# Loading q, k and v for two batches at once, nine rows per partition on all 128 partitions

## Chip, cores, metric

One core of one Trainium2 chip. The metric is device time in microseconds (us), the median of several executions. The runs of the kernel before lie within 0.22% (465.1 to 466.12 us). A run over 1.5% above the fastest of its kernel counts as slow.

## The reference

Attention with a forget gate, then a spectral mix of the result:

```python
# q, k, v: (8 batches, 8 heads, 576, 64) f32;  f: (8, 8, 576)
cum = cumsum(log(clip(f, 1e-4, 1)))
scores = q @ k^T / 8 + cum[..., :, None] - cum[..., None, :]      # causal
x = softmax(scores) @ v            # -> (8, 576, 512), heads side by side
X = rfft(x, axis=1)[:, :64]        # 64 modes
Y[m] = X[m] @ (w_r[m] + 1j * w_i[m])                # 64 x 512 x 512, twice
u = x + irfft(Y, n=576)
out = u + relu(u @ w_ch)
```

The weights `w_r` and `w_i` are 134 MB in f32, q, k and v together 28.3 MB, the output 9.4 MB. Arithmetic is in bf16.

## The kernel before

One step handles one batch and two heads; there are 32 steps. Two streams of loads run side by side. The weights come through GpSimd's software queue, which casts them to bf16 on the way (a packet that reads 2 KB is recorded with 1024 B landed), into a ring of nine tiles of 2 x 4 modes (1 MB in the ring, 2.1 MB read). q, k, v come uncast through SyncE's hardware queue, three staged steps deep.

```python
def emit_w_load(n):                       # 64 tiles in all; first half shown
    wb = wpool.tile([128, 2, MG, D], BF16, tag="wb", name="wb")
    for t, src in enumerate((moe_w_r, moe_w_i)):
        nc.gpsimd.dma_start(wb[:, t, :, :],           # rows of 512 f32: 2 KB packets
            src[g*MG:(g+1)*MG, dc*128:(dc+1)*128, :].rearrange("m p e -> p m e"))
    # ... second half of the tiles: two rows at once, 4 KB packets

def emit_loads(s):                        # RP = 96 partitions, NR = 6 rows each
    dc, b = steps[s]
    for d, src in zip(QKVst[s % STG], (q, k, v)):
        nc.sync.dma_start(d[:, :, :, :].rearrange("p h r d -> p h (r d)"),
            src[b, 2*dc:2*dc+2, :, :].rearrange("h (p r) d -> p h (r d)", r=NR))

def emit_transposes(s):                   # cast, transpose on TensorE, copy out of PSUM
    # ... K: two half-height copies into tiles whose other half is zero
    for h in range(2):
        hs = slice(h*64, h*64+64)
        nc.scalar.copy(KTz[s % NK][h][hs, 0:S].rearrange("c (p r) -> c p r", r=NR),
                       tv[hs, :, :])

# the loop over steps (attention of step s, transposes of s + 1, loads of s + 2)
if s > B:                                 # from step 9 on
    while nmode < (s - B) * NTH // (NS - B):
        emit_modes(nmode)                 # needs weight tile nmode; frees a ring slot
        nmode += 1
        next_w()                          # loads tile nmode + 8
```

After the 32 steps the kernel works through the other half of the weight tiles, and then writes the output in a tail that needs the last tile.

The softmax here doesn't subtract the row's maximum and nothing guards it: scores larger than these inputs give would overflow.

## Time and profile before

| | before |
|---|---|
| time, median | 466.04 us (465.1 to 466.12, the first 3 runs) |
| span of the profiled run | 463.0 us |
| last weight tile landed | 417.4 us |
| tail after it | 45.6 us |
| busy PE / ACT / DVE | 68% / 54% / 53% |

From the page, the span in 40 slices of 11.6 us: busy tenths of ACT and of the 16 DMA engines, and what those moved:

```profile
ACT  4789999999973675469784043442000002104763
...
DMA  8999999999999999999999999999999999982667
GB/s 205 268 268 268 268 268 268 267 267 267 268 266 228 232 258 240 246 217 264 208 206 208 211 212 211 211 211 211 211 211 211 211 211 211 211 161 83 225 245 267
```

The DMA engines are busy to 90% or more in every slice from the second to 405 us, and to 80% or more in the slice in which the weights end, near 417 us. The GB/s line counts what lands; the weights land as half of what was read, so 211 GB/s of weights alone are 422 GB/s read.

The chain that ended last, its pieces around the end of the weights (start, length, what):

```profile
402.75 14.67 DMA wb<-in_moe_w_i_dram
417.46 0.55 PE A L130 x14
418.46 0.61 PE pl L674 x4
...
456.34 1.11 DVEq L784
```

The last matmuls of the modes start 40 ns after the last landing (402.75 + 14.67 = 417.42). From there PE, ACT and DVE write the output until the span ends. Before it, the chain is nearly all landings of weights and channel weights (88% of the span is DMA).

Two stretches, with busy time of each engine, granted clock of TensorE (1 is full speed), DMA share and GB/s landed. The DMA share here adds up packet durations; it goes over 1 because packets overlap in an engine:

```profile
core 0: us, PE busy (x) PEld busy (x) DVE busy (x) ACT busy (x) POOL busy (x), PEclk, DMA share, GB/s
30.00:130.00 100.00, 84.28 (x1538) 66.29 (x1539) 89.52 (x244) 95.09 (x148) 14.83 (x20) 0.97 1.16 268
230.00:250.00 20.00, 16.12 (x329) 13.76 (x326) 15.09 (x44) 14.71 (x24) 5.95 (x8) 0.91 1.24 206
```

Between 30 and 130 us ACT is busy 95% of the time, so attention is close to being bound by ACT there. But the list of waits (total, number, longest) shows who waits afterwards:

```profile
PE A L130 <- DMA wb<-in_moe_w_i_dram: 74.2, 37, 3.5
...
PE A L130 <- DMA wb<-in_moe_w_r_dram: 27.0, 21, 1.6
```

PE waits 101 us for weights. A faster attention would reach these waits earlier.

The q/k/v issues (bytes each and median time to landing), the two queues (packets, MB, share of 16 engines' time), and three groups of work that the change touches (busy us, mean ns of one):

```profile
stq<-in_q_dram SPq DMA_DIRECT2D x32, 288.0 KB, 9.2
stk<-in_k_dram SPq DMA_DIRECT2D x32, 288.0 KB, 8.8
stv<-in_v_dram SPq DMA_DIRECT2D x32, 288.0 KB, 8.7
```

```profile
q0 software_dynamic: 51760, 67.64, 82.4%
q1 hardware_dynamic: 24960, 37.77, 25.7%
```

```profile
L407 ACT COPY KTz<-tp 64x576 bf16<-64x576 bf16 x64 | 42.9, 671 | 7.5 <-PE tp L398 6.6
...
L383 ACT CAST kb<-stk 96x768 bf16<-96x768 f32 x32 | 26.3, 834 | 0.0
...
L453 PE MATMUL ps<-QTs,KTz 128*128 128x448 bf16 x64 | 21.9, 399 | 0.0
```

**What one packet costs.** The trace also records every DMA packet, with queue, size, start and duration. I cut the stretch in which both queues work into slices of 4 us and solved by least squares for the two numbers that make (weight packets x cost + q/k/v packets x cost) fill 4 us of an engine (counts are means over the 16 engines):

```
before: packet kind           packets per engine   ns of an engine   us in all
  weights, 2 KB read                 2080               80              167
  weights, 4 KB read                 1024              156              160
  q, k, v, 1536 B                    1152               73.2             84
recorded durations of a q/k/v packet: 65 ns with no weights about, 78 ns next to weights
```

Cost and duration differ because packets overlap in an engine (the DMA share above is 1.16). The three sums, 411 us, are the 417 us in which DMA is busy, less the start (the first weight packet starts at 3.8 us) and the 4-byte packets of both queues: 4016, one for each transfer in each engine, three quarters of them 22 ns long. I call these completion packets.

### The profile page before, as it was taken

Reading aid. Unit: us, or ns where it says so; the run is one execution under the profiler, and the core shown is the slowest. Engines: PE = TensorE matmul, PEld = TensorE weight load, DVE = VectorE, ACT = ScalarE, POOL = GpSimd, SP = SyncE. Lnnn points to the kernel's source line nnn. Section 1 sums busy time; section 2 is a strip of 40 time slices with the busy share of each in tenths; the row PEclk is TensorE's granted clock in tenths of the full one; section 3 lists DMA queues with packets and bytes.
Section 4 is the critical chain, followed back from the end, with each engine's and each line's share of the span. In section 5 each row is a group of like instructions: output and inputs, shape, how many; then the busy total and the mean of one; then the engine's idle time right before and its main releaser. Section 6 shows DMA issues by size and latency. Waiting matters only on the chain.

```text
span 463.0 us, 11454 instructions
## 1 busy us (share of the span) xinstructions
PE 315.8 (68%) x4845; PEld 224.3 (48%) x4845; DVE 245.0 (53%) x625; ACT 248.0 (54%) x376; POOL 120.9 (26%) x154
## 2 busy tenths in 40 slices
PE   1768778898865673677977599996222248347993
PEld 1446556777654553556766456663122125223441
DVE  7868889999954563358777313321000012105774
ACT  4789999999973675469784043442000002104763
POOL 6111101221112211121222322322322233101884
PEclk9979999999987887579899599998555558657998
DMA  8999999999999999999999999999999999982667
GB/s 205 268 268 268 268 268 268 267 267 267 268 266 228 232 258 240 246 217 264 208 206 208 211 212 211 211 211 211 211 211 211 211 211 211 211 161 83 225 245 267
DMA packets 76852, 106.28 MB, mean 230 GB/s; under 512 B 4032, under 2 KB 55744, under 8 KB 76800
## 3 DMA queue, kind: packets, MB, share of 16 engines
q0 software_dynamic: 51760, 67.64, 82.4%
q1 hardware_dynamic: 24960, 37.77, 25.7%
q8 instruction: 38, 0.62, 0.5%
q10 hardware_dynamic: 80, 0.13, 0.2%
q14 instruction: 14, 0.11, 0.1%
HBM read 163.73 MB, written 9.44 MB: 374 GB/s over the span
## 4 chain that ended last, share of the span: by engine, by line
DMA 88%; PE 6%; ACT 1%; issue 1%; DVE 1%; POOL 1%; DVEq 0%; ACTq 0%; POOLq 0%
DMA wb<-in_moe_w_i_dram 69%; DMA wb<-in_moe_w_r_dram 12%; DMA wch<-in_moe_w_ch_dram 8%; PE pz L703 2%; PE pu L715 1%; PE pz L715 1%; ACT uo L731 1%; PE pu L698 1%; PE pl L678 1%; ACT uo L728 0%; POOL wb L87 0%; DVE uo L732 0%; DVE uo L725 0%; DVEq L784 0%; PE pl L674 0%
## 5 line engine op out<-in xcount | busy, mean ns | idle before, releaser
L130 PE MATMUL A<-XT,wb 128*128 128x16 bf16 x2048 | 77.1, 172 | 101.8 <-DMA wb<-in_moe_w_i_dram 74.2
L130 PEld LDWEIGHTS <-wb 128*128 128x128 bf16 x2048 | 68.4, 100 | 115.3 <-DMA wb<-in_moe_w_i_dram 79.2
L460 ACT ACTIVATE E<-ps 128x1024 bf16<-128x1024 f32 (+1 forms) x128 | 105.6, 855 | 19.1 <-PE ps L453 17.6
L453 PE MATMUL ps<-QTs,KTz 128*128 128x64 bf16 (+4 forms) x384 | 73.1, 303 | 8.7 <-ACT E L460 7.6
L145 DVE TENSOR_TENSOR YT<-A,Yacc 128x128 bf16<-128x128 f32 x24 | 8.8, 368 | 97.1 <-PE A L130 97.1
L87 POOL DMA_DIRECT2D wb<-in_moe_w_r_dram x32 | 24.5, 766 | 113.1 <-DMA wb<-in_moe_w_r_dram 40.0
L487 PE MATMUL pav<-va,E 128*128 128x65 bf16 x960 | 48.1, 202 | 2.8 <-DVE x_all L496 2.0
L407 ACT COPY KTz<-tp 64x576 bf16<-64x576 bf16 x64 | 42.9, 671 | 7.5 <-PE tp L398 6.6
L475 DVE TENSOR_TENSOR E<-E,trimask 128x256 bf16<-128x256 bf16 (+2 forms) x128 | 38.6, 307 | 11.5 <-ACT E L460 10.6
L633 ACT CAST yy<-pyw 128x512 bf16<-128x512 f32 x8 | 4.7, 586 | 74.0 <-PE pyw L626 74.0
L487 PEld LDWEIGHTS <-E 128*128 128x128 bf16 x960 | 41.0, 104 | 5.5 <-DVE x_all L496 2.5
L453 PEld LDWEIGHTS <-KTz 128*128 128x128 bf16 x384 | 32.3, 104 | 21.3 <-issue 14.6
L87 POOL DMA_DIRECT2D wb<-in_moe_w_i_dram x32 | 23.9, 747 | 69.3 <-DMA wb<-in_moe_w_i_dram 68.1
L621 ACT CAST XW<-pxw 128x512 bf16<-128x512 f32 x40 | 22.7, 587 | 35.1 <-PE pxw L614 35.1
L99 POOL DMA_DIRECT2D wb<-in_moe_w_r_dram x33 | 22.7, 687 | 67.7 <-DMA wb<-in_moe_w_r_dram 50.0
L614 PE MATMUL pxw<-wch,yy 128*128 128x512 bf16 x160 | 38.5, 393 | 0.0
L99 POOL DMA_DIRECT2D wb<-in_moe_w_i_dram x33 | 23.0, 697 | 53.0 <-DMA wb<-in_moe_w_i_dram 50.5
L729 POOL TENSOR_TENSOR uo<-uo 64x512 f32<-64x512 f32 (+1 forms) x14 | 25.2, 1811 | 28.6 <-DVE uo L725 25.7
L389 DVE TENSOR_TENSOR vb<-stv,wdec 96x768 bf16<-96x768 f32 x32 | 30.4, 950 | 3.4 <-PE tp L398 3.4
L418 ACT COPY VT<-tp 128x576 bf16<-128x576 bf16 x32 | 20.3, 635 | 20.4 <-PE tp L398 20.3
L496 DVE TENSOR_TENSOR x_all<-pav,rcp 128x384 bf16<-128x384 f32 x64 | 31.0, 484 | 0.5
L413 DVE COPY QTs<-tp 128x576 bf16<-128x576 bf16 x32 | 24.1, 752 | 5.3 <-PE tp L398 4.1
(103 smaller groups left out, 496.4 us busy)
## 6 DMA issues: line engine op xcount, KB each, us to landing
wb<-in_moe_w_r_dram POOLq DMA_DIRECT2D x63, 512.0 KB, 20.3
wb<-in_moe_w_i_dram POOLq DMA_DIRECT2D x63, 512.0 KB, 20.6
stq<-in_q_dram SPq DMA_DIRECT2D x32, 288.0 KB, 9.2
stk<-in_k_dram SPq DMA_DIRECT2D x32, 288.0 KB, 8.8
stv<-in_v_dram SPq DMA_DIRECT2D x32, 288.0 KB, 8.7
out_dram<-uo SPq DMA_DIRECT2D x16, 512.0 KB, 3.1
out_dram<-uo SPq DMA_DIRECT2D x7, 128.0 KB, 2.4
wch<-in_moe_w_ch_dram POOLq DMA_DIRECT2D x1, 512.0 KB, 38.0
```

What stands on the lines that cost most here:

```text
L87: nc.gpsimd.dma_start(wb[:, t, :, :], src[g * MG : (g + 1) * MG, dc * 128 : (dc + 1) * 128, :].rearrange("m p e -> p m e"),)
L99: nc.gpsimd.dma_start(wb[:, t, ms, :], src[g * M2 : (g + 1) * M2, D // 2 : D, :][ms].rearrange("m (p r) e -> p m (r e)", r=2),)
L130: nc.tensor.matmul(A[:, eb, mi, :], lhsT=wb[:, t, mi, r * D + eb * 128 : r * D + (eb + 1) * 128], rhs=XT3[:, m, c0 : c0 + 2 * B], start=(i ...
L389: nc.vector.tensor_tensor(vb[:, :, :, :], stv_[:, :, :, :].rearrange("p h r d -> p r h d"), _strided(wdec6[:, 0, c0 : c0 + 1], [[BH, NR], ...
L407: nc.scalar.copy(KTz[s % NK][h][hs, 0:S].rearrange("c (p r) -> c p r", r=NR), tv[hs, :, :],)
L453: nc.tensor.matmul(ps[:, h, o : o + n], lhsT=KTz[s % NK][h][:, jb * 128 : (jb + 1) * 128], rhs=QT[s][:, jb * 128 + c0 : jb * 128 + c0 + n] ...
L460: nc.scalar.activation(E[:, :, piece * 512 : piece * 512 + w], ps[:, :, 0:w], ACT.Exp, scale=scale,)
L475: nc.vector.tensor_tensor(dg, dg, tr, ALU.mult)
L487: nc.tensor.matmul(pav[:, i, h, :], lhsT=E[:, h, c : c + 128], rhs=va[:, jb, h, :], start=(jb == 0), stop=(jb == sb),)
L496: nc.vector.tensor_tensor(x_all[:, b, sbs[0] : sbs[0] + n, dc * 128 : (dc + 1) * 128].rearrange("p c (h d) -> p c h d", h=2), pav[:, 0:n, ...
L614: nc.tensor.matmul(pxw[:, :], lhsT=xT[:, eb, sb * 128 : (sb + 1) * 128], rhs=wch[:, eb, :], start=(eb == 0), stop=(eb == NDC - 1),)
L729: nc.gpsimd.tensor_tensor(o_sb, o_sb, u_sb, ALU.add)
```

## The change

Intent: use all 128 partitions in loads, casts and transposes, fetch longer runs, and halve the number of loads. A pair of steps now shares one load per tensor: two heads (64 partitions each, nine rows a partition) of two batches. After the transposes the batches lie on the two partition halves. So K need not be padded with zeros, and scores become matmuls of 64 rows. Staging takes the same room (two pairs instead of three steps).

```diff
-    RP = 96
+    RP = 64
     NR = S // RP
+    RG = ((0, 5), (5, 4))
-    STG = 3
+    STG = 2
@@ loads
-            dc, b = steps[s]
-            for d, src in zip(QKVst[s % STG], (q, k, v)):
+            dc, bp, _ = steps[2 * pr]
+            for d, src in zip(QKVst[pr % STG], (k, q, v)):
+                one = src[2 * bp, 2 * dc, :, :]
                 nc.sync.dma_start(
-                    d[:, :, :, :].rearrange("p h r d -> p h (r d)"),
-                    src[b, 2 * dc : 2 * dc + 2, :, :].rearrange(
-                        "h (p r) d -> p h (r d)", r=NR
-                    ),
+                    d[:, :, :, :].rearrange("p b r d -> p b (r d)"),
+                    bass.AP(tensor=one.tensor, offset=one.offset,
+                        ap=[[NR * Dh, 128], [H * S * Dh, 2], [1, NR * Dh]]),
                 )
@@ scores (cut)
-                        lhsT=KTz[s % NK][h][:, jb * 128 : (jb + 1) * 128],
-                        rhs=QT[s][:, jb * 128 + c0 : jb * 128 + c0 + n],
+                        lhsT=KTs[pr % 2][bs, h, jb * 128 : (jb + 1) * 128],
+                        rhs=QT[pr][bs, h, jb * 128 + c0 : jb * 128 + c0 + n],
@@ the loop
-            if s + STG - 1 < NS:
-                emit_loads(s + STG - 1)
-            if s + 1 < NS:
-                emit_transposes(s + 1)
+            pr, h = s // 2, s % 2
+            if h == 0 and pr + STG < NPR:
+                emit_loads(pr + STG)
+            if pr + 1 < NPR:
+                emit_transposes(pr + 1, ("kq", "v")[h])
 # cut: prologue (decay factors in the new layout), casts and copies per pair,
 # attention's output and transforms for two batches
```

More of the change, by code (lines that the diff above doesn't have):

```diff
@@ L160 @@
         qtp = actx.enter_context(tc.tile_pool(name="qtp", bufs=2))
-        vap = actx.enter_context(tc.tile_pool(name="vap", bufs=3))
+        vap = actx.enter_context(tc.tile_pool(name="vap", bufs=2))
         epl = actx.enter_context(tc.tile_pool(name="epl", bufs=1))
@@ L179, with emit_loads @@
         wdec = ssb.tile([128, NSB, BH], BF16, name="wdec")
-        wdec6 = ssb.tile([RP, NR, BH], BF16, name="wdec6")
-        NK, NE = 2, 2
+        wdec9 = ssb.tile([128, NR, B, NDC], BF16, name="wdec9")
+        NE = 2
         QKVst = [
-            [stq.tile([RP, 2, NR, Dh], F32, name=f"st{nm}{i}") for nm in "qkv"]
+            [stq.tile([128, 2, NR, Dh], F32, name=f"st{nm}{i}") for nm in "qkv"]
             for i in range(STG)
         ]
-        VTs = [kt.tile([128, SP], BF16, name=f"VT{i}") for i in range(2)]
-        KTz = [
-            [kt.tile([128, SP], BF16, name=f"KTz{i}_{h}") for h in range(2)]
-            for i in range(NK)
-        ]
-        Es = [epl.tile([128, 2, EW], BF16, name=f"E{i}") for i in range(NE)]
-        steps = [(dc, b) for dc in range(NDC) for b in range(B)]
-        def emit_loads(s):
-            dc, b = steps[s]
-            for d, src in zip(QKVst[s % STG], (q, k, v)):
-                nc.sync.dma_start(
-                    d[:, :, :, :].rearrange("p h r d -> p h (r d)"),
-                    src[b, 2 * dc : 2 * dc + 2, :, :].rearrange(
-                        "h (p r) d -> p h (r d)", r=NR
+        VTs = [kt.tile([128, 2, SP], BF16, name=f"VT{i}") for i in range(2)]
+        KTs = [kt.tile([128, 2, SP], BF16, name=f"KT{i}") for i in range(2)]
+        Es = [epl.tile([128, 2, EW], BF16, name=f"E{i}") for i in range(NE)]
+        steps = [(dc, bp, h) for dc in range(NDC) for bp in range(B // 2) for h in (0, 1)]
+        NPR = len(steps) // 2
+        def emit_loads(pr):
+            dc, bp, _ = steps[2 * pr]
+            for d, src in zip(QKVst[pr % STG], (k, q, v)):
+                one = src[2 * bp, 2 * dc, :, :]
+                nc.sync.dma_start(
+                    d[:, :, :, :].rearrange("p b r d -> p b (r d)"),
+                    bass.AP(
+                        tensor=one.tensor,
+                        offset=one.offset,
+                        ap=[[NR * Dh, 128], [H * S * Dh, 2], [1, NR * Dh]],
                     ),
@@ L224 @@
         nc.sync.dma_start(ft[:], f.rearrange("b h s -> (b h) s"))
-        for s in range(STG - 1):
-            emit_loads(s)
+        for pr in range(STG):
+            emit_loads(pr)
         nc.gpsimd.memset(trimask[:, :], 1.0)
@@ L254 @@
         for t in VTs:
-            nc.vector.memset(t[:, S:SP], 0.0)
-        for pair in KTz:
-            nc.vector.memset(pair[0][64:128, :], 0.0)
-            nc.vector.memset(pair[1][0:64, :], 0.0)
-            nc.vector.memset(pair[0][0:64, S:SP], 0.0)
-            nc.vector.memset(pair[1][64:128, S:SP], 0.0)
+            nc.vector.memset(t[:, :, S:SP], 0.0)
+        for t in KTs:
+            nc.vector.memset(t[:, :, S:SP], 0.0)
         for t in Es:
@@ L266 @@
         nc.scalar.activation(lf[:], ft[:], ACT.Ln)
-        onesS = scratch(BH, S)
+        wide = scratch(128, 2 * S)
+        onesS = wide[:BH, 0:S]
         nc.vector.memset(onesS[:], 1.0)
@@ L278 @@
             )
-        cum6_ps = psT.tile([RP, NR, BH], F32, tag="tr", name="cum6_ps")
-        for r in range(NR):
-            nc.tensor.transpose(
-                cum6_ps[:, r, :],
-                _strided(cum[:, r : r + 1], [[NR, RP]]),
-                ident_f[:BH, :BH],
+        cum2 = wide[:BH, :].rearrange("c (r h p) -> c r h p", r=NR, h=2)
+        for h in range(2):
+            nc.vector.tensor_copy(
+                cum2[:, :, h, :], _strided(cum[:, 0:1], [[1, NR], [NR, RP]])
             )
@@ L313 @@
         nc.vector.memset(wdec[64:128, 4, :], 0.0)
-        bias6 = ftf[:RP, 0 : NR * BH].rearrange("p (r c) -> p r c", r=NR)
-        nc.vector.tensor_tensor(
-            bias6[:, :, :],
-            _strided(Rb[:RP, :], [[0, NR], [1, BH]]),
-            cum6_ps[:, :, :],
-            ALU.subtract,
-        )
-        nc.scalar.activation(wdec6[:, :, :], bias6[:, :, :], ACT.Exp)
+        bias9 = ftf[:, 0 : NR * B * NDC].rearrange(
+            "p (r b c) -> p r b c", r=NR, b=B
+        )
+        for r0, n in RG:
+            cum9_ps = psT.tile([128, 5, BH], F32, tag="tr", name="cum9_ps")
+            for r in range(r0, r0 + n):
+                nc.tensor.transpose(
+                    cum9_ps[:, r - r0, :],
+                    cum2[:, r, :, :].rearrange("c h p -> c (h p)"),
+                    ident_f[:BH, :BH],
+                )
+            for h in range(2):
+                hs = slice(h * 64, h * 64 + 64)
+                nc.vector.tensor_tensor(
+                    bias9[hs, r0 : r0 + n, :, :],
+                    _strided(Rb[hs, h : h + 1], [[0, n], [H, B], [2, NDC]]),
+                    _strided(
+                        cum9_ps[hs, 0, h : h + 1], [[BH, n], [H, B], [2, NDC]]
+                    ),
+                    ALU.subtract,
+                )
+        nc.scalar.activation(wdec9[:, :, :, :], bias9[:, :, :, :], ACT.Exp)
         def emit_basis():
@@ L331, in emit_basis @@
             nc.vector.tensor_copy(m_f[:], m_i[:])
-            ang = scratch(128, 2, NSB, NM)
+            ang = wide[:, 0 : 2 * NSB * NM].rearrange(
+                "p (a b c) -> p a b c", a=2, b=NSB
+            )
             rnd = scratch(128, 2, NSB, NM)
@@ L375 @@
         QT, vaugs = {}, {}
-        def emit_transposes(s):
-            stq_, stk_, stv_ = QKVst[s % STG]
-            dc, b = steps[s]
-            c0 = b * H + 2 * dc
-            kb = qkb.tile([RP, NR, 2, Dh], BF16, tag="kb", name="kb")
-            kv = kb[:, :, :, :].rearrange("p r h d -> p h r d")
-            nc.scalar.copy(kv, stk_[:, :, :, :])
-            qb = qkb.tile([RP, NR, 2, Dh], BF16, tag="qb", name="qb")
-            nc.vector.tensor_copy(
-                qb[:, :, :, :].rearrange("p r h d -> p h r d"), stq_[:, :, :, :]
-            )
-            vb = qkb.tile([RP, NR, 2, Dh], BF16, tag="vb", name="vb", bufs=1)
-            nc.vector.tensor_tensor(
-                vb[:, :, :, :],
-                stv_[:, :, :, :].rearrange("p h r d -> p r h d"),
-                _strided(wdec6[:, 0, c0 : c0 + 1], [[BH, NR], [1, 2], [0, Dh]]),
-                ALU.mult,
-            )
-            for which, src in (("k", kb), ("q", qb), ("v", vb)):
-                tp = psT.tile([128, NR, RP], BF16, tag="tr", name="tp")
-                for r in range(NR):
-                    nc.tensor.transpose(
-                        tp[:, r, :],
-                        src[:, r, :, :].rearrange("p h d -> p (h d)"),
-                        ident_bf[:RP, :RP],
-                    )
-                tv = tp[:, :, :].rearrange("c r p -> c p r")
-                if which == "k":
-                    for h in range(2):
-                        hs = slice(h * 64, h * 64 + 64)
-                        nc.scalar.copy(
-                            KTz[s % NK][h][hs, 0:S].rearrange("c (p r) -> c p r", r=NR),
-                            tv[hs, :, :],
-                        )
-                elif which == "q":
-                    QTs = qtp.tile([128, S], BF16, tag="QT", name="QTs")
-                    nc.vector.tensor_copy(
-                        QTs[:, :].rearrange("c (p r) -> c p r", r=NR), tv
-                    )
-                    QT[s] = QTs
-                else:
-                    nc.scalar.copy(
-                        VTs[s % 2][:, 0:S].rearrange("c (p r) -> c p r", r=NR), tv
-                    )
@@ new lines, in emit_transposes, with rows @@
+        def emit_transposes(pr, what):
+            dc, bp, _ = steps[2 * pr]
+            for which in what:
+                st = QKVst[pr % STG]["kqv".index(which)]
+                sb = qkb.tile([128, NR, 2, Dh], BF16, tag="cb", name=which + "b")
+                flat = sb[:, :, :, :].rearrange("p r b d -> p b r d")
+                if which == "k":
+                    nc.scalar.copy(flat, st[:, :, :, :])
+                elif which == "q":
+                    nc.vector.tensor_copy(flat, st[:, :, :, :])
+                    QT[pr] = qtp.tile([128, 2, S], BF16, tag="QT", name="QTs")
+                else:
+                    nc.vector.tensor_tensor(
+                        sb[:, :, :, :],
+                        st[:, :, :, :].rearrange("p b r d -> p r b d"),
+                        _strided(
+                            wdec9[:, 0, 2 * bp, dc : dc + 1],
+                            [[B * NDC, NR], [NDC, 2], [0, Dh]],
+                        ),
+                        ALU.mult,
+                    )
+                for r0, n in RG:
+                    tp = psT.tile([128, 5, 2, RP], BF16, tag="tr", name="tp")
+                    for r in range(r0, r0 + n):
+                        nc.tensor.transpose(
+                            tp[:, r - r0, :, :].rearrange("c h p -> c (h p)"),
+                            sb[:, r, :, :].rearrange("p b d -> p (b d)"),
+                            ident_bf[:, :],
+                        )
+                    tv = tp[:, 0:n, :, :].rearrange("c r h p -> c h p r")
+                    def rows(t):
+                        return t.rearrange("c h (p r) -> c h p r", r=NR)[
+                            :, :, :, r0 : r0 + n
+                        ]
+                    if which == "k":
+                        nc.scalar.copy(rows(KTs[pr % 2][:, :, 0:S]), tv)
+                    elif which == "q":
+                        nc.vector.tensor_copy(rows(QT[pr][:, :, :]), tv)
+                    else:
+                        nc.scalar.copy(rows(VTs[pr % 2][:, :, 0:S]), tv)
@@ L422, in emit_vback @@
         def emit_vback(s):
-            dc, b = steps[s]
-            c0 = b * H + 2 * dc
+            dc, bp, h = steps[s]
+            c0 = 2 * bp * H + 2 * dc + h
             vp = psT.tile([128, NSB, 2, Dh], BF16, tag="tr", name="vp")
@@ L427, in emit_vback @@
                 nc.tensor.transpose(
-                    vp[:, sc, :, :].rearrange("p h d -> p (h d)"),
-                    VTs[s % 2][:, sc * 128 : (sc + 1) * 128],
+                    vp[:, sc, :, :].rearrange("p b d -> p (b d)"),
+                    VTs[s // 2 % 2][:, h, sc * 128 : (sc + 1) * 128],
                     ident_bf[:, :],
@@ L435, in emit_vback @@
                 va[:, :, :, Dh : Dh + 1],
-                _strided(wdec[:, 0, c0 : c0 + 1], [[BH, NSB], [1, 2], [1, 1]]),
+                _strided(wdec[:, 0, c0 : c0 + 1], [[BH, NSB], [H, 2], [1, 1]]),
             )
@@ L450, in emit_scores @@
             ps = psS.tile([128, 2, 512], F32, tag="sc", name="ps")
-            for h in range(2):
-                for jb, c0, n, o in PIECES[piece]:
+            h, pr = s % 2, s // 2
+            for jb, c0, n, o in PIECES[piece]:
+                for b in range(2):
+                    bs = slice(b * 64, b * 64 + 64)
                     nc.tensor.matmul(
-                        ps[:, h, o : o + n],
-                        lhsT=KTz[s % NK][h][:, jb * 128 : (jb + 1) * 128],
-                        rhs=QT[s][:, jb * 128 + c0 : jb * 128 + c0 + n],
+                        ps[:, b, o : o + n],
+                        lhsT=KTs[pr % 2][bs, h, jb * 128 : (jb + 1) * 128],
+                        rhs=QT[pr][bs, h, jb * 128 + c0 : jb * 128 + c0 + n],
                         start=True,
@@ L477, in emit_av @@
         def emit_av(s, sbs):
-            dc, b = steps[s]
+            dc, bp, hd = steps[s]
             E = Es[s % NE]
@@ L496, in emit_av @@
             nc.vector.tensor_tensor(
-                x_all[:, b, sbs[0] : sbs[0] + n, dc * 128 : (dc + 1) * 128].rearrange(
-                    "p c (h d) -> p c h d", h=2
-                ),
+                x_all[
+                    :,
+                    2 * bp : 2 * bp + 2,
+                    sbs[0] : sbs[0] + n,
+                    dc * 128 + hd * Dh : dc * 128 + (hd + 1) * Dh,
+                ].rearrange("p b c d -> p c b d"),
                 pav[:, 0:n, :, 0:Dh],
@@ L503, in emit_av, with emit_dft @@
             )
-        def emit_dft(s):
-            dc, b = steps[s]
+        def emit_dft(pr):
+            dc, bp, _ = steps[2 * pr]
             if dc == 2:
                 return
-            for c, d0, st in [(dc, dc * 128, 1)] if dc < 2 else [(2, 256, 2), (3, 257, 2)]:
-                if b == 0:
-                    XT3s[c] = xtpool.tile(
-                        [128, NM, 3 * B], BF16, tag="XT3", name=f"XT{c}"
-                    )
-                px = psT.tile([128, NM, 2], F32, tag="tr", name="px")
-                for sb in range(NSB):
-                    nc.tensor.matmul(
-                        px[:, :, :],
-                        lhsT=_strided(x_all[:, b, sb, d0 : d0 + 1], [[st, 128]]),
-                        rhs=bas[:, sb, :, :],
-                        start=(sb == 0),
-                        stop=(sb == NSB - 1),
-                    )
-                XT3 = XT3s[c]
-                nc.vector.tensor_copy(
-                    _strided(XT3[:, 0, B + b : B + b + 1], [[3 * B, NM], [B, 2]]),
-                    px[:, :, :],
-                )
-                nc.scalar.mul(XT3[:, :, b : b + 1], px[:, :, 1:2], -1.0)
+            forms = [(dc, dc * 128, 1)] if dc < 2 else [(2, 256, 2), (3, 257, 2)]
+            for b in (2 * bp, 2 * bp + 1):
+                for c, d0, st in forms:
+                    if b == 0:
+                        XT3s[c] = xtpool.tile(
+                            [128, NM, 3 * B], BF16, tag="XT3", name=f"XT{c}"
+                        )
+                    px = psT.tile([128, NM, 2], F32, tag="tr", name="px")
+                    for sb in range(NSB):
+                        nc.tensor.matmul(
+                            px[:, :, :],
+                            lhsT=_strided(x_all[:, b, sb, d0 : d0 + 1], [[st, 128]]),
+                            rhs=bas[:, sb, :, :],
+                            start=(sb == 0),
+                            stop=(sb == NSB - 1),
+                        )
+                    XT3 = XT3s[c]
+                    nc.vector.tensor_copy(
+                        _strided(XT3[:, 0, B + b : B + b + 1], [[3 * B, NM], [B, 2]]),
+                        px[:, :, :],
+                    )
+                    nc.scalar.mul(XT3[:, :, b : b + 1], px[:, :, 1:2], -1.0)
         NS = len(steps)
@@ L541 @@
         tc.no_sync_barrier()
-        emit_transposes(0)
+        emit_transposes(0, "kqv")
         for s in range(NS + 1):
-            if s + STG - 1 < NS:
-                emit_loads(s + STG - 1)
-            if s + 1 < NS:
-                emit_transposes(s + 1)
+            pr, h = s // 2, s % 2
[3 more added lines that the diff above has]
+                emit_transposes(pr + 1, ("kq", "v")[h])
             if s < NS:
@@ L560 @@
             if s >= 1:
-                emit_dft(s - 1)
                 vaugs.pop(s - 1)
+                if h == 0:
+                    emit_dft(pr - 1)
             if s > B:
```

## The prediction

> **What bounds the kernel now.** DMA, until 417 us of a 463 us span. The chain of waits is 88% DMA, nearly all landings of the weight tiles `wb`; its last DMA piece ends at 417.4 us, then a 46 us tail of PE, ACT and DVE follows. The slices show DMA at 9 tenths throughout. The stage windows show ACT busy 14.7 of 15 us between 60 and 120 us, so attention is close to ACT-bound there; but after 135 us PE waits for weights (74 us on `moe_w_i`, list of waits), so a faster attention only waits longer.
>
> So the time is DMA work before the last weight lands, plus the tail. From the DMA packet records, by queue and size:
> - weights, 2 KB read, 2080 packets per DMA engine. Alone (230-250 us) they land 204.5 GB/s, 80 ns a packet per engine: 167 us.
> - weights, 4 KB read, 1024 per engine, 209.8 GB/s, 156 ns: 160 us.
> - q, k, v: 1536 B, 18432 packets, 1152 per engine. From 15 to 135 us the two queues alternate packet for packet (1101 against 1101 per 10 us), 150 ns a pair, so 70 ns a q/k/v packet: 81 us.
>
> Sum 408 us plus a start at 3.8 us: 412, near the 417 seen.[...]
>
> **What changes on that path.** Bytes do not change (28.3 MB of q, k, v). Packets become 2304 B, 768 per engine. Packet durations before are nearly constant: 1536 B takes 65 ns alone, 78 ns when it alternates with a weight packet; the packets of f, 2304 B too, take 93 ns alone. So 28 ns for 768 B more, and the rest is fixed per packet. Estimate: 70 + 28 = 98 ns, times 768 = 75 us instead of 81: 5 us less. Half as many loads also means 48 fewer completion packets per engine, about 20 ns each: up to 1 us.
>
> A rival: 96 partitions[...]; then the gain would be larger[...]. The constant durations speak against contention, so I give it little weight.
>
> **What changes off that path.** Per pair of steps, K's four half-height copies (671 ns each) become two full-height ones (about 1.3 us in all, estimate), the casts of K go from 2 x 834 ns to about 1.2 us: ACT saves about 0.9 us of 6 us a step, DVE about 0.5. Scores in 64-row tiles shorten PE (73 us of score matmuls), which isn't limiting. Attention will run about 5 us a step instead of 6 until weights hold it up; modes begin near 65 us instead of 78. Then PE waits more for weights. The weight ring should not run dry: before, its first nine tiles had landed only at 96 us. The prologue grows by 1-2 us, hidden by DMA. The tail is untouched.
>
> **Prediction.** 466 - 5.5 = 460.5 us, range 456 to 464.5. Faster by over 2%: 0.13; same: 0.83; slower: 0.04.
>
> **What would show it.** DMA at 9 tenths until 405-415 us; last weight landing 5-6 us earlier; tail still 45-46 us; q/k/v packets about 104 ns when they alternate; ACT busy time down by about 30 us; PE's waits on weights up by tens of us.
>
> **What would make it wrong.** [...]Cost proportional to bytes: no change. DMA gaps, where the bigger, burstier loads leave attention late and the ring full: slower. A tail that moves with the granted clock.

The sums stand as 167 + 160 + 81 = 408 us, with the start 412 us; and 466 - 5.5 = 460.5 us, the 5.5 being 5 us of q/k/v packets and part of the up to 1 us of completion packets. The rival's point is that a load costs more on 96 partitions than on 128. "The constant durations" are those of the q/k/v packets: 17623 of 18432 took 78 ns.

## The result

| | before | after |
|---|---|---|
| time, median | 465.95 us (4 runs) | 458.7 us (458.57 to 458.98, 4 runs) |
| span of the profiled run | 463.0 | 457.1 |
| last mode matmuls start | 417.46 | 411.26 |
| from there to the end | 45.6 | 45.8 |
| busy ACT / DVE / PE, us | 248.0 / 245.0 / 315.8 | 227.8 / 235.6 / 311.7 |

The ratio is 0.9855 (95% interval 0.984 to 0.9869). Ratios are the mean time of one kernel's fast runs over that of the other's of the same rounds, so not quite the ratio of the medians quoted. This is 1.45% less, within the 2% that I called "same". The result is right.

The same lines of the kernel after. (Its tiles are named by the order q, k, v but loaded in the order k, q, v, so `stq` holds k.) First the slices:

```profile
ACT  3699999898836536573872133442000012005772
...
DMA  8999999999999999999999999999999999972677
GB/s 229 275 294 294 294 294 283 275 274 274 274 252 239 276 218 273 215 223 206 207 207 208 211 211 211 211 211 211 211 211 211 211 211 212 212 143 93 219 253 264
```

DMA is still full until the slice in which the weights end. The landed rate in the slices with most q/k/v rose from 268 to 294 GB/s.

```profile
396.48 14.73 DMA wb<-in_moe_w_i_dram
411.26 0.56 PE A L131 x14
412.26 0.61 PE pl L694 x4
...
450.30 1.11 DVEq L804
```

```profile
30.00:130.00 100.00, 80.95 (x1452) 61.41 (x1450) 86.36 (x233) 89.10 (x129) 15.32 (x20) 0.98 1.14 282
230.00:250.00 20.00, 14.33 (x303) 11.40 (x299) 13.57 (x40) 9.73 (x16) 5.61 (x8) 0.89 1.23 207
```

```profile
PE A L131 <- DMA wb<-in_moe_w_i_dram: 71.8, 33, 4.8
...
PE A L131 <- DMA wb<-in_moe_w_r_dram: 26.2, 21, 3.4
```

The last landing is 6.2 us earlier and the tail is as long as before. ACT has 6 us less to do between 30 and 130 us, yet PE waits for weights as long as before, 98 us.

```profile
stq<-in_k_dram SPq DMA_DIRECT2D x16, 576.0 KB, 9.2
stk<-in_q_dram SPq DMA_DIRECT2D x16, 576.0 KB, 7.9
stv<-in_v_dram SPq DMA_DIRECT2D x16, 576.0 KB, 8.4
```

```profile
q0 software_dynamic: 51760, 67.64, 83.8%
q1 hardware_dynamic: 18048, 37.77, 24.0%
```

```profile
L397 ACT CAST kb<-stq 128x1152 bf16<-128x1152 f32 x16 | 18.8, 1177 | 8.2 <-PE tp L414 8.2
...
L466 PE MATMUL ps<-QTs,KT 64*128 64x448 bf16 x64 | 13.4, 390 | 0.0
...
L427 ACT COPY KT<-tp 128x640 bf16<-128x640 bf16 x16 | 12.3, 766 | 9.7 <-PE tp L414 9.7
L427 ACT COPY KT<-tp 128x512 bf16<-128x512 bf16 x16 | 11.9, 745 | 5.2 <-PE tp L414 5.2
```

The packets:

```
q/k/v packets          per engine   ns of an engine   us in all   duration (no weights / next to weights)
before, 1536 B            1152           73.2           84.4          65 / 78 ns
after,  2304 B             768          101.3           77.8          93 / 106 ns
```

The q/k/v packets take 6.6 us less of every DMA engine, and the last weight lands 6.2 us earlier. That is nearly all of the gain.

### The profile page after: what moved, and what is told of

Same layout as the page of the kernel before. It is cut to its first block, busy times and chain, and to the rows that moved or that the text cites. A ratio compares the mean times of both kernels' runs of the same rounds, so it can differ in the third digit from the quotient of the medians.

```text
span 457.1 us, 10986 instructions
## 1 busy us (share of the span) xinstructions
PE 311.7 (68%) x4704; PEld 213.6 (47%) x4704; DVE 235.6 (52%) x592; ACT 227.8 (50%) x329; POOL 121.1 (26%) x154
## 4 chain that ended last, share of the span: by engine, by line
DMA 88%; PE 6%; ACT 1%; issue 1%; DVE 1%; POOL 1%; DVEq 0%; ACTq 0%; POOLq 0%
DMA wb<-in_moe_w_i_dram 66%; DMA wb<-in_moe_w_r_dram 13%; DMA wch<-in_moe_w_ch_dram 8%; PE pz L723 2%; PE pu L735 2%; PE pz L735 1%; ACT uo L751 1%; PE pu L718 1%; PE pl L698 1%; ACT uo L748 0%; POOL wb L88 0%; DVE uo L752 0%; DVE uo L745 0%; DVEq L804 0%; PE pl L694 0%
## 5 line engine op out<-in xcount | busy, mean ns | idle before, releaser
L131 PE MATMUL A<-XT,wb 128*128 128x16 bf16 x2048 | 72.1, 172 | 98.4 <-DMA wb<-in_moe_w_i_dram 71.8
L473 ACT ACTIVATE E<-ps 128x1024 bf16<-128x1024 f32 (+1 forms) x128 | 104.0, 873 | 26.9 <-PE ps L466 26.0
L131 PEld LDWEIGHTS <-wb 128*128 128x128 bf16 x2048 | 63.3, 99 | 113.7 <-DMA wb<-in_moe_w_i_dram 76.3
L466 PE MATMUL ps<-QTs,KT 64*128 64x64 bf16 (+4 forms) x384 | 51.2, 304 | 7.6 <-ACT E L473 6.8
L500 PEld LDWEIGHTS <-E 128*128 128x128 bf16 x960 | 39.8, 104 | 10.8 <-issue 6.4
L88 POOL DMA_DIRECT2D wb<-in_moe_w_i_dram x32 | 24.1, 753 | 71.4 <-DMA wb<-in_moe_w_i_dram 65.0
L427 ACT COPY KT<-tp 128x640 bf16<-128x640 bf16 (+1 forms) x32 | 23.0, 755 | 14.9 <-PE tp L414 14.9
L466 PEld LDWEIGHTS <-KT 64*128 64x128 bf16 x384 | 18.0, 96 | 20.8 <-issue 10.8
L542 DVE CAST XT<-px 128x128 bf16<-128x128 f32 x32 | 20.8, 808 | 9.0 <-PE px L534 8.8
L546 ACT ACTIVATE XT<-px 128x64 bf16<-128x64 f32 x32 | 14.6, 467 | 20.1 <-DVE XT L542 17.6
L634 PEld LDWEIGHTS <-yy 128*128 128x128 bf16 x160 | 15.1, 100 | 19.5 <-DVE yy L630 5.9
```

The costliest lines, as they stand in the source:

```text
L88: nc.gpsimd.dma_start(wb[:, t, :, :], src[g * MG : (g + 1) * MG, dc * 128 : (dc + 1) * 128, :].rearrange("m p e -> p m e"),)
L131: nc.tensor.matmul(A[:, eb, mi, :], lhsT=wb[:, t, mi, r * D + eb * 128 : r * D + (eb + 1) * 128], rhs=XT3[:, m, c0 : c0 + 2 * B], start=(i ...
L427: nc.scalar.copy(rows(KTs[pr % 2][:, :, 0:S]), tv)
L466: nc.tensor.matmul(ps[:, b, o : o + n], lhsT=KTs[pr % 2][bs, h, jb * 128 : (jb + 1) * 128], rhs=QT[pr][bs, h, jb * 128 + c0 : jb * 128 + c ...
L473: nc.scalar.activation(E[:, :, piece * 512 : piece * 512 + w], ps[:, :, 0:w], ACT.Exp, scale=scale,)
L500: nc.tensor.matmul(pav[:, i, h, :], lhsT=E[:, h, c : c + 128], rhs=va[:, jb, h, :], start=(jb == 0), stop=(jb == sb),)
```

## Experiments

The theory, N: the time is the sum of DMA packets up to the last weight plus a fixed tail, and a q/k/v packet next to weights costs a fixed amount besides its bytes, so fewer packets are the gain. From the two costs above: (101.3 - 73.2) ns for 768 B is 36.6 ns per 1000 B, which leaves 17 ns fixed. Rival P: a packet costs more on 96 partitions than on 128, whatever the mechanism, and 128 partitions are the gain. Rival C: the lighter attention arithmetic is the gain.

### e1: the kernel after with packets as small as before

```diff
-                    d[:, :, :, :].rearrange("p b r d -> p b (r d)"),
+                    d[:, :, :, :].rearrange("p b r d -> p (b r d)").rearrange("p (c e) -> p c e", c=3),
-                        ap=[[NR * Dh, 128], [H * S * Dh, 2], [1, NR * Dh]],
+                        ap=[[384, 128], [128 * 384, 3], [1, 384]],
```

> The kernel after, but each load fetches its bytes as 1536 B packets (three per partition) on all 128 partitions: 1152 packets per DMA engine as before, wrong result on purpose. Theory N (number of packets: a fixed cost of some 16 ns for each q/k/v packet next to a weight packet; 73 ns for 1536 B, 101.5 ns for 2304 B): the whole gain goes, last weight landing near 417 us, 464 to 466 us. Rival P (96 partitions[...], 128 cure it): stays at 458.7 us. Rival C (the lighter attention arithmetic gives the gain): stays at 458.7 us.

Measured: 465.32 us against 465.32 for the kernel before (ratio 0.9998, interval 0.9981 to 1.0015). A packet cost 72.8 ns. The hardware queue's line and the end of the weights:

```profile
q1 hardware_dynamic: 24192, 37.77, 25.4%
```

```profile
417.75 0.56 PE A L131 x14
```

The whole gain is gone, with all of the change's arithmetic and all 128 partitions still in place. Both rivals fall for this kernel: partitions are worth 73.2 - 72.8 = 0.4 ns a packet, 0.5 us in all, and the arithmetic nothing that shows.

### e2: the kernel after with packets twice as large

```diff
-                        ap=[[NR * Dh, 128], [H * S * Dh, 2], [1, NR * Dh]],
+                        ap=[[1152, 128], [1, 1152]],       # and a flat destination
```

> The kernel after, each load as one 4608 B packet per partition: 384 packets per engine, wrong result on purpose. Theory N: 187 ns each, 72 us instead of 78, so about 6 us less than the kernel after: 452.5 us (451 to 454). Rivals P and C: 458.7 us.

Measured: 453.36 us (ratio 0.9746). A packet cost 186.9 ns, 71.8 us in all; the straight line through the other two sizes gives 101.3 + 3 x 28.1 = 185.6 ns.

```profile
q1 hardware_dynamic: 11904, 37.77, 22.6%
```

```profile
405.48 0.56 PE A L131 x14
```

The kernel obeys the packet count further than the change took it. Its output is wrong, which doesn't matter for the time. A right kernel with such loads would need another layout (18 rows per partition).

### e3: the kernel before with half its packets

```diff
-                    d[:, :, :, :].rearrange("p h r d -> p h (r d)"),
+                    d[:, :, :, :].rearrange("p h r d -> p (h r d)"),
-                        "h (p r) d -> p h (r d)", r=NR
+                        "h (p r) d -> (h p) (r d)", r=2 * NR
```

> The kernel before, all its arithmetic and 96 partitions, each load as one 3072 B packet per partition instead of two of 1536 B, wrong result on purpose. Theory N: 576 packets of 130 ns, 75 us instead of 84: about 8.7 us less than before, 457.3 us (456 to 459). Rivals P and C: 466 us as before.

Measured: 459.62 us (ratio 0.9878, interval 0.9859 to 0.9896). This misses the expected range by 0.6 us but is 5.7 us faster than before, on 96 partitions and with the old arithmetic. A packet cost 132.0 ns instead of 130 (76.0 us in all), and between 8 and 16 us the packets filled only about 87% of the DMA engines' time, some 1 us more. Why 2 ns more is not settled; 96 partitions may have a small part in it.

### e4: the kernel before with the packets of the kernel after

```diff
-            [stq.tile([RP, 2, NR, Dh], F32, name=f"st{nm}{i}") for nm in "qkv"]
+            [stq.tile([128, 768], F32, name=f"st{nm}{i}") for nm in "qkv"]
-                    d[:, :, :, :].rearrange("p h r d -> p h (r d)"),
+                    d[:, 0:576],
-                        "h (p r) d -> p h (r d)", r=NR
+                        "h (p r) d -> (h p) (r d)", r=9
 # the arithmetic reads [96, 768] of the tile; columns 576 on are set to zero once
```

> The kernel before, all its arithmetic, with the packets of the kernel after: 2304 B on 128 partitions, still one load per step and tensor, wrong result on purpose. Theory N: 78.5 us of q/k/v instead of 84: 460 us (459 to 461). Rival P: 458.7 to 460 us. Rival C: 466 us.

Measured: 458.68 us, where the kernel after has 458.7 (ratio to before 0.9863). A packet cost 101.7 ns. The time is 0.3 us below the expected range, at the lower end of what rival P would give here, so this run doesn't tell N from P; e1, e2 and e3 do. The end of the weights:

```profile
411.14 0.56 PE A L130 x14
```

The load alone, with every bit of the old arithmetic, gives the whole gain. e1 and e4 together close the question for rival C.

### e5 and e6: one queue instead of two

What is the fixed cost of 17 ns? The durations suggest a place: 65 or 93 ns alone, exactly 13 more (78, 106) next to weights. Do the two queues take turns packet by packet? The counts fit that: from 45 to 55 us of the kernel after, 923 records of the weights' queue stand against 925 of the other (891 and 866 without the 4-byte completion packets). Equal counts alone would also fit turns of several packets each; but 96% of the q/k/v packets of the kernel before (17623 of 18432) had the 78 ns of one next to weights, so I take it that nearly every one has a weight packet beside it. The order itself was not shown. Theory A: the cost is paid at that alternation. In one queue, I expected, the packets of a load come in runs.

```diff
-                nc.sync.dma_start(
+                nc.gpsimd.dma_start(
@@ weights: three tiles first, then one a step, then the channel weights
-        for n in range(NRING):
+        for n in range(NFIRST):        # NFIRST = 3
@@ loop
+            if NFIRST + s < NRING:
+                emit_w_load(NFIRST + s)
 # e6 besides: staging tiles in BF16, so that the DMA casts
```

> The kernel after, with q, k, v issued from GpSimd like the weights, so that all packets stand in one queue and come in runs instead of alternating (right result; the first weight tiles are spread over the first steps so that q, k, v do not queue behind all nine). Theory A (the fixed 16 ns of a q/k/v packet is paid where an engine changes between the queues): a 2304 B packet falls from 101.5 to about 90 ns, 69 us instead of 78, last weight landing near 402 us, 450 us (448 to 453). Rival I (the cost belongs to packets that are not cast, in whatever order): 458.7 us. Rival S ([...]a blocked load holds back weights): gaps in the DMA, slower than 458.7 us.

> As the run before, and the DMA casts q, k, v to bf16 as it does the weights (v is then rounded once more; else a right result). Theory A and rival I both give about 90 ns for a packet that reads 2304 B and 450 us; where the run before stays at 458.7 us and this one falls to 450 us, rival I is right. Rival S: gaps and slower.

Measured: e5 459.39 us, e6 457.48 to 459.7 in three fast runs; both results right. e6's profiled run was slow (533.57 us at a granted clock of 1.0); I have no explanation and draw nothing from it after 250 us. The expected 450 us were missed, but not because the packets stayed dear: 4608 B (one record holds two 2304 B pieces here) cost 177 ns, 88.5 a piece instead of 101.3, and e6's cast pieces 90.5. q/k/v took 68 us, 10 less than after. (459.39 us is also the number of rival I; the cost of an uncast packet, and e7 below, speak against it.)

Not all of these 10 us belong to the queue, for the records also became larger. e2 had records of 4608 B too, as many as e5, in their own queue, and there one cost 186.9 ns. So larger records explain 6 of the 10 us (77.8 to 71.8), and the one queue the other 4. The durations agree: before any weights came, e2's records took 178 ns as a rule, and next to weights 191 (5822 of 6144); in one queue 178 is the rule again, in two thirds of e5's records. So most of the 13 ns that a neighbour in the other queue adds are gone.

e5's window from 82 to 102 us, and GpSimd's timeline, show where the 10 us went (columns as above; in the timeline start and length in us, then the wait before it):

```profile
82.00:102.00 20.00, 16.98 (x300) 13.05 (x298) 17.43 (x49) 18.32 (x27) 6.08 (x9) 0.93 0.75 202
```

```profile
63.97 0.77 POOL L568 DMA_DIRECT2D wch<-in_moe_w_ch_dram  x1 [0.44 <-DMA stv<-in_v_dram]
66.62 0.70 POOL L198 DMA_DIRECT2D stq<-in_k_dram  x1 [1.88 <-ACT VT L431]
...
81.53 0.70 POOL L198 DMA_DIRECT2D stk<-in_q_dram  x1 [4.05 <-DVE qb L399]
...
89.02 0.70 POOL L198 DMA_DIRECT2D stq<-in_k_dram  x1 [1.62 <-ACT kb L397]
93.56 0.72 POOL L198 DMA_DIRECT2D stk<-in_q_dram  x1 [3.84 <-DVE qb L399]
94.70 0.75 POOL L88 DMA_DIRECT2D wb<-in_moe_w_r_dram  x1 [0.42 <-PE tp L414]
```

The DMA share is 0.75 there, against 1.1 to 1.2 elsewhere. All nine weight tiles and the channel weights had been issued by 64 us; until the first modes freed a slot at 94.7 us, GpSimd had only q/k/v loads to issue, which wait for attention. The ring was full too early: a gap of my own making.

### e7 and e8: one queue, weights spread out

```diff
-        NFIRST = 3
+        NFIRST = 2
@@ loop
-            if NFIRST + s < NRING:
-                emit_w_load(NFIRST + s)
+            if h == 0 and nload < NRING + nmode:
+                next_w()
 # channel weights at step 20; e8: cast in the DMA, three staged pairs
```

> The one-queue kernel (q, k, v uncast, from GpSimd), with the weight tiles spread: two at first, then one every second step until the ring is full, and the channel weights at step 20. In the first one-queue run a 4608 B pair of q/k/v packets cost 177 ns per engine (68 us in all, 10 us less than the kernel after), but the DMA stood mostly idle from 82 to 102 us, because all nine tiles had landed before the first modes freed a slot, which gave some 10 us back. Theory A: without that gap the last weight lands near 401 us and the time is 449 us (447 to 453). If the 10 us are lost elsewhere[...], 455 to 460 us with other gaps.

> The same with the cast in the DMA, and three staged pairs instead of two, since they take half the room. 90.5 ns a packet, 69.5 us: 450 us (448 to 454) if there are no gaps. It tells whether deeper staging closes what gaps the other run still has.

Measured: e7 451.07 us (450.24 to 456.63, ratio 0.9723), e8 451.31 us (450.93 to 452.32, ratio 0.971, interval 0.9692 to 0.9727); both results right. e7's window at the same place:

```profile
82.00:102.00 20.00, 18.68 (x372) 14.66 (x370) 17.75 (x52) 17.51 (x26) 8.14 (x11) 0.75 1.21 237
```

The gap is closed, the last modes start at 403.6 us in both, and both kernels beat before and after (but e2, with two queues and as few records, by only 2 us: 453.36 us, last modes at 405.48): e8 is 7.4 us below the kernel after and steadier than e7. e7's slowest run is the profiled one; its granted clock was 0.686 and its tail 51 us instead of 46.

### e9, e10, e11: does the change matter in one queue?

If theory A holds, the nine-row load has little to save in one queue. So I gave the kernel before one queue.

```diff
 # e9: the kernel before, 96 partitions, 1536 B pieces
-                nc.sync.dma_start(
+                nc.gpsimd.dma_start(
 # and weights spread as in e7
```

> The kernel before (96 partitions, six rows, all its arithmetic) with q, k, v issued from GpSimd, and the weight tiles spread as in the faster one-queue kernels; right result. If the fixed cost belongs to alternating queues (theory A), a 1536 B packet costs here about 61 ns instead of 73, some 70 to 72 us in all, nearly the same as with 2304 B, and the time is 453 us (451 to 456): most of what nine rows gain disappears, because the cost they saved is not there. If the cost belongs to each q/k/v packet whatever the order, it stays near 465 us, 7 us or more behind the one-queue kernel of nine rows at 451 us, or more with gaps.

Measured: 488.15 us, slower than before (ratio 1.05); its two fast runs 480.96 and 486.53 us (the other two, near 490, count as slow by the rule of 1.5%). A clear miss: 4608 B of q/k/v cost about 270 ns instead of 177 (254 if a weight packet is held at the 80 ns of the other runs). Their durations were spread (a quarter under 191 ns, a quarter over 295), where e7 has 178 ns in over three quarters of its records. I took spread durations for a sign of contention, and rival P came back. Two more runs separate 96 partitions from small pieces.

```diff
 # e10: e7 with 1536 B pieces on 128 partitions (the edit of e1)
 # e11: e9 with 2304 B pieces on 128 partitions (the edit of e4)
```

> The faster one-queue kernel (nine-row arithmetic), its loads fetched as 1536 B pieces on 128 partitions, wrong result on purpose. In the kernel before with one queue, 4608 B of q/k/v cost an engine 270 ns with durations spread from 178 to over 320, against a nearly constant 178 for the nine-row one. If the 96 partitions do that[...]: here 178 to 190 ns, 451 to 453 us. If the 1536 B pieces do it: about 270 ns, and 480 us or more.

> The kernel before with all its arithmetic, one queue, weights spread as in the run that was slow, but 2304 B on 128 partitions, wrong result on purpose. If the 96 partitions were the cause: constant durations, 178 ns per 4608 B, 451 to 454 us. If its arithmetic or its 96 smaller loads were the cause: slow as before, 480 us or more. If the 1536 B pieces were: 451 to 454 here, and slow in the other run.

Measured: e10 453.0 us (184.7 ns per 4608 B, so 61.6 a piece), e11 454.29 us (about 186 ns; a few stalls blur this fit). The upper end of e11's range was 454. e9 and e11 in the same stretch:

```profile
120.00:240.00 120.00, 79.19 (x1369) 65.97 (x1377) 66.03 (x175) 68.72 (x96) 47.25 (x67) 0.74 1.18 232
```

```profile
120.00:240.00 120.00, 85.34 (x1676) 70.40 (x1674) 76.13 (x206) 77.87 (x112) 52.02 (x78) 0.81 1.18 249
```

The DMA engines are equally busy, and e9 lands less. Against e7, small pieces on 128 partitions cost 2 us in one queue (e10; three of them share a record of 4608 B, so there are no more records), and the old arithmetic 3 us (e11). Neither comes near e9's 30 us, so 96 partitions are what is left to make e9 slow. No run has 96 partitions with larger pieces in one queue, so a need for both together isn't excluded. Nor does any run show by what mechanism 96 partitions would do it; measured is the cost, 270/184.7 = 1.46 times that of e10's equal pieces.

All runs (uncast pieces in the shared queue are joined in records of 4608 B; the others are records of their own):

| run | load, queue | ns per piece | q/k/v, us | time, us |
|---|---|---|---|---|
| before | 96 x 1536 B, own | 73.2 | 84.4 | 465.95 |
| after | 128 x 2304 B, own | 101.3 | 77.8 | 458.7 |
| e1 | 128 x 1536 B, own | 72.8 | 83.9 | 465.32 |
| e2 | 128 x 4608 B, own | 186.9 | 71.8 | 453.36 |
| e3 | 96 x 3072 B, own | 132.0 | 76.0 | 459.62 |
| e4 | 128 x 2304 B, own, old arithmetic | 101.7 | 78.1 | 458.68 |
| e5 | 128 x 2304 B, shared, gap | 88.5 | 68.0 | 459.39 |
| e6 | 128 x 2304 B cast, shared, gap | 90.5 | 69.5 | 457.48 to 459.7 (fast runs) |
| e7 | 128 x 2304 B, shared | 89.2 | 68.5 | 451.07 |
| e8 | 128 x 2304 B cast, shared | 90.2 | 69.3 | 451.31 |
| e9 | 96 x 1536 B, shared | 90 | 103.7 | 480.96, 486.53 (fast runs) |
| e10 | 128 x 1536 B, shared | 61.6 | 70.9 | 453.0 |
| e11 | 128 x 2304 B, shared, old arithmetic | 93 | 71.4 | 454.29 |

## Why the prediction was right

- **The bound.** Right. Time is DMA up to the last weight plus the tail: the last modes moved by 6.2 us and the tail by 0.2.
- **The size.** 460.5 us predicted, 458.7 measured, within 456 to 464.5. Predicted costs were 70 and 98 ns a packet, measured 73.2 and 101.3. Both were 3 ns low. The equal counts (1101 against 1101) include 4-byte completion packets; of data, only about 1017 q/k/v packets came with 1067 weight packets in 10 us, and (160000 - 1067 x 80) / 1017 gives 73 ns instead of 70. The difference hardly suffered: 81 - 75 plus up to 1 us for completions, against 84.4 - 77.8 = 6.6 us. The microsecond for completions isn't seen: e4 has as many completion packets as before (1920, the kernel after 1152) and the time of the kernel after. The ratio's interval means 6.1 to 7.5 us, so there may be up to another microsecond that the packets do not explain.
- **Fixed cost per packet, not partitions.** Right for this kernel (e1, e2, e3, e4). Durations next to weights were predicted as "about 104 ns" and were 106.
- **The reason for the fixed cost** was not in the prediction. At equal records of 4608 B, one queue took 8.5 to 10 ns off (186.9 in e2, 178.4 in e7, 177 in e5), about half of the 17 ns. The costs per piece fell further (72.8 to 61.6 ns for 1536 B, 101.3 to 88.5 for 2304 B) because pieces then share a record: e10's three cost 184.7 ns together, about as much as e2's single record. Whether the part that the queue takes off is the change of queue or the change between cast and uncast packets stays open, since one queue has fewer of both.
- **Rival P given "little weight".** Right where the queues alternate, and I would have carried it too far: in one queue 96 partitions cost over 20 us (e9 against e11).
- **Attention's pace.** Wrong: modes were to begin "near 65 us instead of 78" and began at 76.7. The failed step is "attention will run about 5 us a step": from its first exponential to the sixteenth step's, a step took 5.5 us instead of 6.2, and the first exponential came at 26.8 instead of 19.8 us, after a longer prologue (predicted to grow "by 1-2 us") and behind first casts, transposes and copies of twice the size. It cost nothing because DMA was full all the while.
- **ACT down "about 30 us".** It was 20. The K copies (42.9 to 24.2 us) and K casts (26.3 to 18.8) fell as they should, but two V copies of 5 and 4 rows cost 1.52 us a pair where two of six rows had cost 1.27.
- **Score matmuls of 64 rows "shorten PE".** Right: PE was busy with them for 51.2 us instead of 73.1. One alone takes about as long as before (390 ns against 399 at 448 columns).
- **PE's waits for weights "up by tens of us".** Wrong: 101 to 98 us. Attention started later and the weights came earlier, which is a likely reason; no run tests it.

## What to carry to other kernels

When DMA is full for nine tenths of the span, cost each kind of packet from the trace and add them up: the sum foretold every alternating run here to 2.5 us, while 20 us of ACT time were worth nothing. Where loads of two queues alternate, cut the number of packets (e2, 453.36 us), or put them into one queue (e7, 451.07 us, which joins pieces into larger records as well); but then spread the weights so that the queue never waits on attention alone, and use all 128 partitions. A tuning that costs nothing under one bottleneck (96 partitions) cost some 6% once q, k, v shared the weights' queue (e9's fast runs against e11).
